# Attention and two MoE layers on one core: other places for the weight conversions, the q/k split, M's first block and the last output

## The chip, the core and the metric

The kernel runs on one core of a Trainium2 chip. The metric is the device time of one execution in microseconds (us). The median of three runs before the change is 732.38 us (731.66 to 733.02).

Five engines work in parallel, each with its own queue of instructions that it takes in order: PE (TensorE, matmuls), DVE (VectorE), ACT (ScalarE), POOL (GpSimd) and SP (SyncE), which here issues the DMAs. An instruction that waits holds up everything behind it in its queue.

## The reference

```python
# attention: B=4, H=8, S=576, D=64
cum = np.cumsum(np.maximum(s, 0.0), axis=-1)
bias = -(cum[:, :, :, None] - cum[:, :, None, :])
scores = np.where(causal, -1e9, q @ k.T / 8 + np.minimum(bias, 0.0))
attn = softmax(scores) @ v
# first MoE: 2304 tokens of 512, DF=1024
x = attn.reshape(2304, 512)
h = (x @ w1) * (x @ w2) @ w3
x = h @ w_out
# second MoE
h = x @ w_in
solu = h * softmax(h)
ln = (solu - mean(solu)) / sqrt(var(solu) + 1e-6) * g_ln
out = ln @ w_out2
```

All is float32. Accuracy is kept by splitting a float32 number into a high and a low word and adding three products (high x high, high x low, low x high).

## The kernel before

**Stages.** From 0 to some 390 us attention and the products of the first MoE with w1 and w2 run together. The program is written in 36 steps. A step takes one head h: its scores (`qk_part`, one large tile of 576 columns with `lmask` and four smaller ones of 448, 64, 320 and 192 with `wmask`), whose row maxima DVE takes out of PSUM (L186) and whose exponentials ACT takes (L190); the normalisation (`normalise`, L218 to L228); the transposes of head h-2 (`tr_part`) with evictions to PT (L93 on ACT, L95 on DVE); and, every other step, the product with v (`av_parts`). Steps 8 and 9 have no head, steps 10 and 11 no transposes. From step 10 on, blocks of the first MoE fill the step (`ab_unit`): block a = x@w1 for 128 of the 1024 columns f and half a batch, twelve matmuls of 128x288, copied to a_sb by ACT (L315), and block b = x@w2, which DVE multiplies by a_sb into g_sb (L323). PSUM tiles of one 512-column bank come from a pool (from step 11 on psF, six banks), those of two banks from another (psE).

**Weights.** The weights come as raw words. A chunk of 512 KB is loaded into one of two `stage` buffers (L384). Its conversion (`to_f32`, `split_w`) is s0 on ACT (L340), three passes on DVE (L346, L347, L351), the high word on ACT (L93, W<-stage) and the low word on DVE (L98, W<-stage,W). A buffer is free for the next load when the low word is written. The chunks come in the order w1(0), w2(0), w1(1), w2(1), ..., of the column blocks f = 0 to 7. `pump(n)` issues n conversions; `PUMP` says how many in which step: one in steps 3, 5, 6 and 16, two in each of steps 10 to 15. After that come chunks of w_in and of the last w_out (steps 22 to 33).

**q and k.** For heads from 8 on `split_qk(h+1)` splits q and k of the next head into words: ACT writes the high word (QK<-qk), SP copies it (L159), POOL subtracts (L98, 64x1152).

**Order.** The program is recorded and then put into the engines' queues by a scheduler that takes what is ready by its own estimates, the earlier written first. `tc.issue_after(i)` holds an instruction back until i has been issued. A conversion is held back behind the instructions in `behind`: before, the maximum and the exponential of the step's large score tile.

**Later stages.** From 390 us M = w3 @ w_out is formed in eight blocks (`m_unit`, 24 matmuls of 128x512), from w3's chunks, whose words are w3h and w3l. M's PSUM tiles come from a pool opened when psF is closed, that is when the last g_sb has been read out of it. DVE and ACT write M's words MH and ML, and convert the words of w_in's combinations (IB11 to IT4) and of g. Then x = M.g, the second MoE's h (`h_pair`), the norm, and the output (`out_unit`, 48 matmuls of 128x512, L836; a tile of 128 rows is evicted by ACT, L841, and sent off by SP, L842).

## Time and profile before

| what | value |
|---|---|
| median of 3 runs | 732.38 us |
| the profiled execution | 732.8 us, its span 731.1 us |
| mean granted clock of PE | 0.995 |
| DVE, ACT | 507.7 us (69%), 470.4 us (64%) |
| POOL | 95.2 us (13%) |
| PE idle in 20 to 40, 40 to 60 us | 0.55, 2.28 us |
| 60 to 80, 80 to 100, 100 to 120, 120 to 140 us | 0.29, 2.19, 0.24, 2.62 us |
| 140 to 380 us | 0 of 240 |
| 380 to 400, 400 to 420, 420 to 440 us | 2.24, 0, 0.61 us |
| 440 to 700 us | 0 of 260 |
| DMA share in 400 to 420 us | 1.03 (380 GB/s) |

The span is the stretch from the first to the last event of the profiled execution; 1.7 us of its time lie around it. The idle times are 20 us, or the window, less PE's busy time in it. PE's busy time counts overlapping matmuls once. The granted clock is the share of PE's full speed that it was given in a window; its levels are 1.2 and 2.4 GHz. "Idle before" in a row is the time in which the engine stood just before the instruction, and behind the arrow is what ended it.

### The profile page before, as it was taken

The numbers are of one execution on the slowest core, as the hardware profiler recorded it, in microseconds if no ns is written. First come the engines' busy times: TensorE is split into PE (matmuls) and PEld (weight loads), VectorE is DVE, ScalarE is ACT, GpSimd is POOL, SyncE is SP. The second block draws the span as 40 slices with busy tenths as digits, with TensorE's granted clock in tenths as the row PEclk, the third lists the DMA queues.
The fourth block names the chain that finished last, engine by engine and source line by source line (L and its number), as shares of the span: only waits on it lengthen the run. The fifth ranks groups of instructions, "written<-read, shape, count | busy, mean of one in ns | idle before, by whom it ended". The sixth has DMA issues, their size and how long they took to land.

```text
span 731.1 us, 12896 instructions
## 1 busy us (share of the span) xinstructions
PE 714.2 (98%) x4618; PEld 631.5 (86%) x4618; DVE 507.7 (69%) x1251; ACT 470.4 (64%) x977; POOL 95.2 (13%) x88
## 2 busy tenths in 40 slices
PE   9989998999999999999998999999999999999997
PEld 6669888889899999999997889988888988888886
DVE  7996989898777887822777966675747366563651
ACT  7996878798676777822544735576737465563742
POOL 3051322234121221000000000001000000000000
PEclk9999999999999999999999999999999999999999
DMA  5644555555476655514566933153324252302311
GB/s 124 190 135 132 156 164 146 164 148 127 140 205 184 207 164 175 179 62 161 185 204 201 378 114 101 59 116 87 79 66 102 45 133 68 87 19 68 66 36 43
DMA packets 79827, 95.50 MB, mean 131 GB/s; under 512 B 41418, under 2 KB 52682, under 8 KB 79764
## 3 DMA queue, kind: packets, MB, share of 16 engines
q1 hardware_dynamic: 79764, 94.69, 44.5%
q8 instruction: 36, 0.59, 0.3%
q14 instruction: 27, 0.22, 0.1%
HBM read 59.04 MB, written 20.14 MB: 108 GB/s over the span
## 4 chain that ended last, share of the span: by engine, by line
PE 81%; DVE 9%; DMA 5%; ACT 2%; issue 2%; SPq 0%; DVEq 0%; ACTq 0%
PE x L710 14%; PE o L836 14%; PE a L303 12%; PE b L303 11%; PE av L275 6%; PE hX L742 5%; PE tr L247 5%; DMA stage<-in_w_dram 4%; PE hZ L742 3%; PE sc L178 2%; PE sc L177 2%; PE hW L742 2%; PE hY L742 2%; DVE stage L351 2%; PE sc L169 1%
## 5 line engine op out<-in xcount | busy, mean ns | idle before, releaser
L190 ACT ACTIVATE P<-P,STAT 64x64 f32<-64x64 f32 (+4 forms) x160 | 88.5, 556 | 22.9 <-DVE STAT L186 22.3
L98 POOL TENSOR_TENSOR QK<-qk,QK 64x1152 fp32r<-64x1152 f32 x24 | 66.2, 2759 | 172.9 <-ACT QK L93 172.8
L710 PE MATMUL x<-gl,MH 128*128 128x256 f32 x288 | 80.4, 279 | 0.0
L710 PE MATMUL x<-gh,ML 128*128 128x256 f32 x288 | 80.2, 279 | 0.0
L710 PE MATMUL x<-gh,MH 128*128 128x256 f32 x288 | 79.9, 279 | 0.0
L303 PE MATMUL b<-xT0h,W 128*128 128x288 f32 x256 | 58.4, 301 | 3.5 <-DVE W L98 2.1
L303 PE MATMUL a<-xT0h,W 128*128 128x288 f32 x256 | 59.2, 306 | 0.0
L247 PE MATMUL tr<-ident,P 128*128 128x128 f32 x416 | 54.4, 275 | 3.5 <-DVE STAT L186 2.7
L303 PE MATMUL a<-xT1h,W 128*128 128x288 f32 x256 | 57.6, 300 | 0.0
L836 PE MATMUL o<-OH,lh 128*128 128x512 f32 x144 | 57.0, 396 | 0.2 <-DVE ll L98 0.2
L836 PE MATMUL o<-OH,ll 128*128 128x512 f32 x144 | 57.0, 396 | 0.0
L836 PE MATMUL o<-OL,lh 128*128 128x512 f32 x144 | 57.0, 396 | 0.0
L303 PE MATMUL b<-xT1h,W 128*128 128x288 f32 x256 | 56.4, 295 | 0.0
L710 PEld LDWEIGHTS x<-gl,MH 128*128 128x128 f32 x288 | 54.1, 188 | 1.5 <-DVE gl L98 0.2
L710 PEld LDWEIGHTS x<-gh,MH 128*128 128x128 f32 x288 | 53.9, 188 | 1.1
L710 PEld LDWEIGHTS x<-gh,ML 128*128 128x128 f32 x288 | 54.0, 188 | 0.9
L806 DVE COPY lt<-turned 128x2048 uint16<-128x2048 uint16 x16 | 22.0, 1373 | 45.4 <-DMA turned<-half 45.4
L247 PEld LDWEIGHTS tr<-ident,P 128*128 128x128 f32 x416 | 46.8, 141 | 5.4 <-issue 1.6
L323 DVE TENSOR_TENSOR g_sb<-b,a_sb 128x288 f32<-128x288 f32 x64 | 28.7, 450 | 31.6 <-PE b L303 21.5
L340 ACT ACTIVATE stage<-stage 128x512 f32<-128x512 f32 x56 | 37.1, 679 | 20.5 <-DMA stage<-in_w_dram 18.7
L226 ACT ACTIVATE P<-P,STAT 128x576 f32<-128x576 f32 x64 | 42.7, 717 | 10.5 <-DVE STAT L219 10.4
L315 ACT ACTIVATE a_sb<-a 128x288 f32<-128x288 f32 x64 | 25.7, 403 | 36.3 <-PE a L303 36.0
(191 smaller groups left out, 1984.1 us busy)
## 6 DMA issues: line engine op xcount, KB each, us to landing
stage<-in_w_dram SPq DMA_DIRECT2D x32, 512.0 KB
g_scr<-g_sb SPq DMA_DIRECT2D x32, 288.0 KB
stage<-in_wo_dram SPq DMA_DIRECT2D x16, 512.0 KB
qk<-in_qk_dram SPq DMA_DIRECT2D x24, 288.0 KB
QK<-QK SPq DMA_DIRECT2D x24, 288.0 KB
gl<-g_scr SPq DMA_DIRECT2D x24, 256.0 KB
wf<-wf_scr SPq DMA_DIRECT2D x22, 256.0 KB
out_dram<-o SPq DMA_DIRECT2D x18, 256.0 KB
```

Of the source, the lines that this page charges most:

```text
L98: eng.tensor_tensor(out=dst, in0=src, in1=hi_.bitcast(F32), op=ALU.subtract)
L190: ex = nc.scalar.activation(out=dst, in_=dst, func=AF.Exp, bias=st[0:rows, ti:ti + 1], scale=-1.0, accum_out=st[0:rows, 5 + ti:6 + ti],)
L226: nc.scalar.activation(out=dst, in_=src, func=AF.Copy, scale=r)
L247: last_tr[0] = nc.tensor.transpose(ps[:, 128 * n:128 * n + 128], pt[:, o:o + 128], ident)
L275: nc.tensor.matmul(st["ps"][64 * e:64 * e + 64, 448 + c0:448 + c1], vr[:, j, e], PT[(2 * p + e) % 4][:, o + c0:o + c1], **kw,)
L303: nc.tensor.matmul(ps, w_[:, c, fs], x_[:, c, sl], start=(c == 0 and w_ is WH and x_ is XH), stop=(c == KC - 1 and w_ is WL),)
L315: ab_last[0] = nc.scalar.activation(out=a_sb, in_=ps, func=AF.Copy).ins
L323: ab_last[1] = nc.vector.tensor_tensor(out=g[:, sl], in0=ps, in1=st["a"], op=ALU.mult).ins
L340: nc.scalar.activation(out=high.bitcast(F32), in_=high.bitcast(F32), func=AF.Copy, scale=2.0 ** -112)
L710: last = nc.tensor.matmul(ps[:, a], w_[:, k, m * 128:m * 128 + 128], g_[:, k % 2], start=(k == 0 and w_ is MH and g_ is GH), stop=(k == KF ...
L742: last_h[0] = nc.tensor.matmul(ps, x_[:, k], w_[:, k], start=first and k == 0 and x_ is XH and w_ is WH, stop=k == 1 and x_ is XL, skip_gr ...
L836: nc.tensor.matmul(ps, l_[:, k], w_[:, k], start=(k == 0 and l_ is LH and w_ is OH), stop=(k == KF - 1 and l_ is LL),)
```

## The change

There are four edits.

- **Conversions.** `behind[0]` is now the maximum of the last score tile of the step so far. The step's first conversion is written behind all score tiles (it was written behind the large one), the others behind the transposes, and these are held back behind the last two evictions of transposes (`last_ev`), one on each of ACT and DVE, instead of the score maximum.
- **Split.** `split_qk(h+1)` is written ahead of the scores of head h instead of at the end of the step.
- **M.** The first block of M takes its PSUM tile from psE, which stays open; psE is now kept at the right end and is closed before the second MoE, where psG, with the tiles X and Y of `h_pair`, takes its banks.
- **Output.** The last tile of 128 rows is computed, evicted and sent in two halves of 256 columns.

```diff
     def hi(dst, src, eng=None):
         if eng is None:
-            nc.scalar.activation(out=dst, in_=src, func=AF.Copy)
-        else:
-            eng.tensor_copy(out=dst, in_=src)
+            return nc.scalar.activation(out=dst, in_=src, func=AF.Copy)
+        return eng.tensor_copy(out=dst, in_=src)
...
         if ti == 0:
             behind[:] = [mx.ins, ex.ins]
+        behind[0] = mx.ins
...
         def evict(dst, src):
             cnt[0] += 1
-            hi(dst, src, PCOPY[cnt[0] % len(PCOPY)])
+            last_ev[cnt[0] % 2] = hi(dst, src, PCOPY[cnt[0] % len(PCOPY)]).ins
...
         if st == 11:
             ps_ctx.close()
             PSP[:] = [
-                ps_ctx.enter_context(tc.tile_pool(name="psE", bufs=1, space=PSUM)),
+                big_ctx.enter_context(tc.tile_pool(name="psE", bufs=1, space=PSUM, side="right")),
                 ps_ctx.enter_context(tc.tile_pool(name="psF", bufs=6, space=PSUM)),
             ]
...
             if NQ <= h + 2 < NH:
                 load_head(h + 2)
+            if h + 1 < NH:
+                split_qk(h + 1)
             qk_part(h, 0)
-        if st > 1:
-            pump(PUMP.get(st, 0))
-        if h is not None:
             qk_part(h, 1)
             qk_part(h, 2)
+        slots = PUMP.get(st, 0)
+        if slots:
+            pump(1)
         F(FS)
         if h is not None:
             normalise(h)
         if ph is not None:
             for part in range(4):
                 tr_part(ph, part)
+        if slots > 1:
+            behind[:] = last_ev
+            pump(slots - 1)
...
-            if h + 1 < NH:
-                split_qk(h + 1)
             if h + 3 < NQ:
...
     def m_unit(f):
-        ps = smalltile("m")
+        ps = smalltile("m") if f else bigtile("m")[:, 0]
...
     ps_ctx.close()
-    PSP[:] = [
-        ctx.enter_context(tc.tile_pool(name="psC", bufs=1, space=PSUM)),
-        ctx.enter_context(tc.tile_pool(name="psD", bufs=4, space=PSUM)),
-    ]
+    psp = {}
+    psp["Z"] = psp["W"] = ctx.enter_context(tc.tile_pool(name="psC", bufs=1, space=PSUM))
+    PSP[1] = ctx.enter_context(tc.tile_pool(name="psD", bufs=4, space=PSUM))
...
     def out_unit(t):
         LH, LL = lt_t.pop(t)
-        ps = smalltile("o")
-        for k in range(KF):
...
+        last = None
+        for c0, c1 in ((0, DM),) if t < NT - 1 else ((0, DM // 2), (DM // 2, DM)):
+            ps = smalltile("o")[:, 0:c1 - c0]
+            with ExitStack() as order:
+                if last is not None:
+                    order.enter_context(tc.issue_after(last.ins))
+                for k in range(KF):
+                    for l_, w_ in ((LH, OH), (LH, OL), (LL, OH)):
+                        last = nc.tensor.matmul(
+                            ps, l_[:, k], w_[:, k, c0:c1],
+                            start=(k == 0 and l_ is LH and w_ is OH), stop=(k == KF - 1 and l_ is LL),
+                        )
+            nc.scalar.activation(out=o[:, c0:c1], in_=ps, func=AF.Copy)
+            nc.sync.dma_start(out=out[t * 128:t * 128 + 128, c0:c1], in_=o[:, c0:c1])
...
+    big_ctx.close()
+    psp["X"] = psp["Y"] = ctx.enter_context(tc.tile_pool(name="psG", bufs=1, space=PSUM, side="right"))
```

What this makes of the queues is shown at three places on DVE, in the stretch from 70 to 120 us. In the names, stage_n is a buffer with a chunk, W01 and W11 are low words of w1, W03 and W13 low words of w2, sc_n a score tile, tr_n a transposed one.

The first place, DVE before, behind the second g_sb of the first MoE: stage_758 holds w2(2), stage_766 holds w1(3).

```order
L323 TENSOR_TENSOR g_sb_814<-b_843,a_sb_829 128x288
L186 ISA P_898,STAT1_117<-sc_899,lmask_109 128x576
L186 ISA STAT1_117 128x1
L346 TENSOR_SCALAR stage_758<-stage_758 128x512
L323 TENSOR_TENSOR g_sb_886<-b_873,a_sb_871 128x288
L347 SCALAR_TENSOR_TENSOR stage_758<-stage_758 128x512
L346 TENSOR_SCALAR stage_766<-stage_766 128x512
```

The same place after; stage_779 holds w2(2), stage_839 holds w1(3).

```order
L325 TENSOR_TENSOR g_sb_809<-b_843,a_sb_824 128x288
L348 TENSOR_SCALAR stage_839<-stage_839 128x512
L325 TENSOR_TENSOR g_sb_886<-b_873,a_sb_871 128x288
L349 SCALAR_TENSOR_TENSOR stage_839<-stage_839 128x512
L353 SCALAR_TENSOR_TENSOR stage_839<-stage_839 128x512
L186 ISA P_901,STAT1_117<-sc_902,lmask_109 128x576
```

The first pass over a chunk came from w2(2), behind a large maximum; it now comes from w1(3), ahead of it, and a g_sb follows.

The second place, DVE before, where the low word of w2(2) is written.

```order
L186 ISA STAT2_118 128x1
L186 ISA P_956,STAT2_118<-sc_989,wmask_108 128x192
L186 ISA STAT2_118 128x1
L351 SCALAR_TENSOR_TENSOR stage_766<-stage_766 128x512
L98 TENSOR_TENSOR W03_125<-stage_758,W02_124 128x4x128
L323 TENSOR_TENSOR g_sb_886<-b_1013,a_sb_1011 128x288
```

The same after; stage_933 holds w2(3).

```order
L186 ISA P_1128,STAT3_119<-sc_1129,lmask_109 128x576
L186 ISA STAT3_119 128x1
L219 TENSOR_SCALAR STAT2_118<-STAT2_118 128x5
L220 RECIPROCAL STAT2_118<-STAT2_118 128x5
L349 SCALAR_TENSOR_TENSOR stage_933<-stage_933 128x512
L229 TENSOR_SCALAR P_959<-P_959,STAT2_118 128x320
L229 TENSOR_SCALAR P_959<-P_959,STAT2_118 128x192
L98 TENSOR_TENSOR W03_125<-stage_779,W02_124 128x4x128
L353 SCALAR_TENSOR_TENSOR stage_933<-stage_933 128x512
L229 TENSOR_SCALAR P_959<-P_959,STAT2_118 64x64
L95 COPY PT0_112<-tr_1051 128x128
L325 TENSOR_TENSOR g_sb_1091<-b_1078,a_sb_1036 128x288
```

The low word of w2(2) stood ahead of the g_sb of b_1013. It now stands behind that g_sb (b_1008 in the new names, which stands eight rows above this piece), behind a large maximum and behind the second pass over w2(3), and ahead of the g_sb of the next block.

The third place, DVE before, at the first pass over w1(6) (stage_1147); stage_1139 holds w2(5).

```order
L186 ISA P_1390,STAT1_117<-sc_1423,wmask_108 128x192
L186 ISA STAT1_117 128x1
L218 TENSOR_SCALAR STAT0_116<-STAT0_116 128x5
L347 SCALAR_TENSOR_TENSOR stage_1139<-stage_1139 128x512
L219 RECIPROCAL STAT0_116<-STAT0_116 128x5
L346 TENSOR_SCALAR stage_1147<-stage_1147 128x512
L351 SCALAR_TENSOR_TENSOR stage_1139<-stage_1139 128x512
```

The same after, where stage_1198 holds w1(6), stage_1160 w2(5) and stage_1074 w1(5).

```order
L348 TENSOR_SCALAR stage_1160<-stage_1160 128x512
L98 TENSOR_TENSOR W11_127<-stage_1074,W10_126 128x4x128
L325 TENSOR_TENSOR g_sb_1286<-b_1343,a_sb_1301 128x288
L186 ISA P_1224,STAT0_116<-sc_1225,lmask_109 128x576
L186 ISA STAT0_116 128x1
L348 TENSOR_SCALAR stage_1198<-stage_1198 128x512
L325 TENSOR_TENSOR g_sb_1386<-b_1373,a_sb_1371 128x288
L186 ISA P_1393,STAT1_117<-sc_1401,wmask_108 128x448
```

The first pass over w1(6) stood behind the four smaller score tiles and the second pass over w2(5). It now stands ahead of these and of a g_sb, three instructions behind the low word of w1(5).

On PE the new order writes two matmuls of the b block of f = 2, then a whole a block, and then the other ten. M's first block stands directly behind the last b block, as before, but no longer shares a pool with it. The third block's ML and one low word of T3 (IT3l) change places with passes over w3 on DVE.

## Rows read from the trace of the kernel before

**Rows 1.** The page, part 1: busy us, share of the span, instructions by engine.

```profile
PE 714.2 (98%) x4618; PEld 631.5 (86%) x4618; DVE 507.7 (69%) x1251; ACT 470.4 (64%) x977; POOL 95.2 (13%) x88
```

**Rows 2.** Timeline of PE: start us, us, engine, line, op, tiles, [idle before <-releaser].

```profile
73.42 0.47 PE L177 MATMUL sc<-QK 128*128 128x448 f32 x1 [0.29 <-DVE g_sb L323]
...
83.53 0.40 PE L303 MATMUL b<-xT0h,W 128*128 128x288 f32 x1 [0.67 <-DVE g_sb L323]
...
85.22 0.29 PE L303 MATMUL a<-xT0h,W 128*128 128x288 f32 x1
...
89.03 0.39 PE L177 MATMUL sc<-QK 128*128 128x320 f32 x1
...
89.61 0.38 PE L247 MATMUL tr<-ident,P 128*128 128x128 f32 x2
...
92.67 0.52 PE L247 MATMUL tr<-ident,P 128*128 128x128 f32 x3 [1.40 <-DVE STAT L186]
...
120.53 0.40 PE L303 MATMUL b<-xT0h,W 128*128 128x288 f32 x1 [0.76 <-ACT W L93]
...
123.70 0.54 PE L303 MATMUL b<-xT0h,W 128*128 128x288 f32 x2 [2.09 <-DVE W L98]
...
391.99 0.50 PE L626 MATMUL m<-WOH,w3h 128*128 128x512 f32 x1 [2.24 <-DVE g_sb L323]
...
428.71 0.50 PE L626 MATMUL m<-WOH,w3h 128*128 128x512 f32 x1 [0.61 <-ACT w3h L93]
```

**Rows 3.** Windows of 4 us: length, busy us by engine, PEclk, DMA share, GB/s.

```profile
92.00:96.00 4.00, 3.21 (x15) 3.00 (x16) 4.00 (x14) 3.95 (x11) 2.03 (x1) 0.74 0.36 109
...
124.00:128.00 4.00, 4.00 (x21) 4.00 (x20) 4.00 (x19) 3.61 (x9) 0.00 (x0) 0.58 0.77 219
```

**Rows 4.** Timeline of DVE, 72 to 123 us: weight chunks and g_sb.

```profile
72.58 0.43 DVE L346 TENSOR_SCALAR stage<-stage 128x512 uint32<-128x512 uint32 x1 [1.90 <-DMA stage<-in_w_dram]
...
73.93 0.43 DVE L346 TENSOR_SCALAR stage<-stage 128x512 uint32<-128x512 uint32 x1
...
87.37 0.69 DVE L98 TENSOR_TENSOR W<-stage,W 128x512 fp32r<-128x512 f32 x1
...
91.42 0.43 DVE L346 TENSOR_SCALAR stage<-stage 128x512 uint32<-128x512 uint32 x1 [0.59 <-DMA stage<-in_w_dram]
...
109.64 0.69 DVE L98 TENSOR_TENSOR W<-stage,W 128x512 fp32r<-128x512 f32 x1 [0.84 <-ACT W L93]
...
111.26 0.45 DVE L323 TENSOR_TENSOR g_sb<-b,a_sb 128x288 f32<-128x288 f32 x1
...
116.59 0.43 DVE L346 TENSOR_SCALAR stage<-stage 128x512 uint32<-128x512 uint32 x1 [1.72 <-DMA stage<-in_w_dram]
...
116.94 0.68 DVE L351 SCALAR_TENSOR_TENSOR stage<-stage 128x512 uint32<-128x512 uint32 x1
...
122.97 0.68 DVE L98 TENSOR_TENSOR W<-stage,W 128x512 fp32r<-128x512 f32 x1
```

**Rows 5.** Timeline of POOL and of DVE, 119 to 123 us.

```profile
119.86 2.64 POOL L98 TENSOR_TENSOR QK<-qk,QK 64x1152 fp32r<-64x1152 f32 x1 [5.71 <-ACT QK L93]
...
120.74 2.31 DVE L351 SCALAR_TENSOR_TENSOR stage<-stage 128x512 uint32<-128x512 uint32 x1
```

**Rows 6.** Timeline of SP: the load of w1(6).

```profile
110.72 0.36 SPq L384 DMA_DIRECT2D stage<-in_w_dram  x1
```

**Rows 7.** Timeline of DVE and ACT, 410 to 429 us.

```profile
410.36 0.43 DVE L346 TENSOR_SCALAR stage<-stage 128x512 uint32<-128x512 uint32 x1 [0.47 <-DMA stage<-in_w_dram]
...
424.52 0.68 DVE L98 TENSOR_TENSOR IT3l<-wf,IT3h 128x512 fp32r<-128x512 f32 x1
...
427.98 0.68 ACT L93 ACTIVATE w3h<-stage 128x512 fp32r<-128x512 f32 x1 [0.85 <-DVE stage L351]
```

**Rows 8.** Timeline of ACT at the end; groups by form on ACT.

```profile
727.40 0.60 ACT L841 ACTIVATE o<-o 128x512 f32<-128x512 f32 x1 [5.00 <-PE o L836]
...
L93 ACT ACTIVATE PT<-tr 128x256 f32<-128x256 f32 x32 | 12.0, 374 | 0.0
```

More of the change, by code (lines that the diff above doesn't have):

```diff
@@ L63, in tile_attention_moe @@
     ps_ctx = ExitStack()
+    big_ctx = ExitStack()
     PSP = [
@@ L261, in tile_attention_moe @@
     last_tr = [None]
+    last_ev = [None, None]
     cnt = [0]
@@ L851, in h_pair @@
         h0, h1 = ln_t[t0][0], ln_t[t1][0]
-        X, Y, Z, W = (PSP[0].tile([128, HD], F32, tag=n, name=f"h{n}") for n in "XYZW")
+        X, Y, Z, W = (psp[n].tile([128, HD], F32, tag=n, name=f"h{n}") for n in "XYZW")
         h_mm(X, "A11", "B11", True)
```

7 lines of the change are left out of this document (removed).

## The prediction

> **What bounds the kernel now.** I read the page first. TensorE (PE) is busy for 714.2 of 731.1 us, so only PE's idle places can be won or lost [rows 1]. The second view is PE's timeline, row by row where a bracket stands. Up to 52 us DVE and ACT are full and have the same work ahead of each of PE's waits after the change, so I leave that stage as it is. Behind it there are seven places that the change can touch: 0.29, 0.67, 1.40, 0.76 and 2.09 us between 73 and 124 us, 2.24 us at 392 and 0.61 us at 428.71 [rows 2]. The third is the granted clock in 4 us windows. It stands at 0.74 in 92 to 96 and at 0.58 in 124 to 128, right behind the idle places of 92.67 and 123.70: for part of these windows PE ran at 1.2 instead of 2.4 GHz [rows 3]. From 0.58, half clock lasted (1 - 0.58) x 4 / 0.5 = 3.4 us and cost half of that, 1.7 us. The 2.24 us at 392 brought no fall that the page's slices show, so a wait's length does not tell it alone, and I price the clock in the bounds only.
>
> The fourth view is VectorE's (DVE's) timeline, to see what made PE wait. Two things do. The first instruction of a weight chunk (L346) waits for the chunk's DMA, and whatever stands behind it in DVE's queue waits too: at 91.42 it waited 0.59 us, and the score maxima behind it are what PE wanted at 92.67 [rows 4]. And DVE is slow while GpSimd (POOL) splits q and k: the L351 at 120.74 took 2.31 us beside the split of 119.86 to 122.50, and the chunk's last instruction, for which PE waited, came at 122.97 [rows 4, 5].
>
> I name chunks by weight and block: w2(2) is the chunk of w2 for the third block, f = 2. PE needs w1(f) and then w2(f), in the order of f.
>
> **The conversions, 57 to 124 us.** No conversion is added or removed; in steps 10 to 15 there are two in a step, and their places change.
>
> First, the order of the pair. Before, w2(2) was converted ahead of w1(3). Now the step's second conversion stands behind evictions only, step 11 has none of its own, and w1(3) goes first, though SP still issues w2(2)'s load ahead of w1(3)'s. In the trace, the first of these two loads released DVE at 72.58, the second at 73.93 [rows 4]. DVE's queue now meets the later one first, with g_sb behind it, for which PE waited at 73.42. So g_sb moves by up to 73.93 - 72.58 = 1.35 us.
>
> More comes from w2(2) itself. PE uses its low half in the block that began at 83.53. Now the low half is written behind the next step's large maximum and one more pass of w2(3), next to the place where w1(3)'s low half stood, 87.37 to 88.06 [rows 4]. PE goes on with two matmuls of the block and the next block meanwhile (the new order puts them there). A block took 85.22 - 83.53 = 1.69 us [rows 2]. At 88.06 there remain ten of twelve matmuls, 1.41 us, and before they would have been reached at 85.22 + 1.69 - 1.41 = 85.5. PE is late by 2.6 us there; the bounds are 0 (w2(2) is written where it was) and 2.6 + 2.64, one split of POOL in the way [rows 5].
>
> Second, w1(4). Its first instruction waited for the load until 91.42. It now stands ahead of a g_sb (0.45 us by its row at 111.26, some 0.4 where instructions overlap) and a low half (0.69 at 87.37, some 0.6), and the maxima stand behind all three. So PE can go on at about 92.67 + 0.4 + 0.6 = 93.7, if the load lands as before; coming 2.6 us late it would be there at 92.67 - 1.40 + 2.6 = 93.9. The old wait swallows most of the lateness, and about 1.2 us are left. Bounds: -1.4 (the wait vanishes) to +5.
>
> Third, w2(5), for which PE waited at 120.53 and 123.70. Before, w1(6)'s first instruction came behind a g_sb, four maxima and more, and still waited 1.72 us for its DMA, issued at 110.72 and landed at 116.6 [rows 4, 6]. That load can start only when w1(5)'s low half is written, since there are two buffers. Now the instruction stands three places behind that low half. If the load lands at the same time, all that ran from 111.26 to 116.59 - 1.72 = 114.87 (g_sb, four maxima, the sum's reciprocal, w2(5)'s second pass) runs behind it: 3.6 us. w2(5)'s third pass, at 116.94 before, comes 3.6 us later, and its high and low halves with it. The low half also gets one large maximum more ahead of it and one pass less, which is even. PE gets 0.58 us of score matmuls into the wait (89.03 to 89.61 are the same shapes) [rows 2]. So PE goes on 3.6 - 0.6 = 3.0 us later than at 123.70. PE waits for DVE's chain there, so the 1.2 us of before are in this, not beside it.
>
> What hides how much of this is open. For it speaks that w1(5)'s high half no longer stands behind an a_sb copy on ScalarE (ACT), so the 0.84 us that DVE waited for it at 109.64 may go and the load of w1(6) start as much earlier; against it, that w2(5)'s first instruction, which waits for a DMA, now stands ahead of that low half. I take the full +3.0. The bounds: below, every wait of 73 to 124 us goes, 0.29 + 0.67 + 1.40 + 0.76 + 2.09 = 5.2, and both half-clock stretches, 3.4, together -8.6; above, 3.0 plus one blocked split, +5.6.
>
> **Splitting q and k at the step's head.** The same number of splits (POOL's part 2.64 us each) start earlier; SP's copy goes with them. It costs nothing by itself: POOL is busy 13% of the span (its share on the page's first line) [rows 1]. What it moves is the stretch in which DVE is slow. The row at 120.74 shows a DVE pass with two SBUF inputs beside POOL's split: 2.31 us, where such a pass took 0.68 at 116.94 [rows 4, 5]. The Trainium skill, "SBUF — State Buffer", section "Who interferes with whom", says that a DVE instruction with two SBUF inputs and a GpSimd instruction that reads SBUF share a port pair, and that the first to issue keeps it for its whole length; the trace agrees with its 2.31 us. By it an earlier split frees nothing: it only blocks other passes. I count no gain for it; with a gain at 120.74 of 2.31 - 0.68 = 1.6 the sum would be 1.6 lower.
>
> **M's first block.** It no longer waits for the last g_sb, so PE starts 2.24 us earlier [rows 2]. What is late next is w3: at 428.71 PE waited for w3h, written at 427.98 to 428.66, so an early start alone would only lengthen that wait. In the new order two DVE instructions that stood ahead of that chunk's third pass are elsewhere: the ML of the third block is written before DVE's wait for a load at 410.36, and one low half of T3 goes behind. Each takes 0.68 us, some 0.6 where they overlap, in a stretch where DVE runs back to back [rows 7]. So w3h comes 1.2 us earlier, and PE with it: -1.2. Bounds: 0 and -(2.24 + 0.61) = -2.85. Behind 429 us PE has no idle place up to 715, so the gain holds to the end.
>
> **The last output.** Two halves of 256 columns. The PE time stays (48 matmuls half as long). The last eviction took 0.60 us for 512 columns; for 256 columns from PSUM the evictions to PT have 0.374 [rows 8]: -0.2. The last transfer has half the bytes; from the eviction's end at 728.0 to the end of the span pass 3.1 us, and no row splits them into fixed and by size. I take 0.15 (bounds 0 and 1.5). Together -0.35.
>
> **The sum.** +3.0 - 1.2 - 0.35 = +1.45 us on the profiled 732.8 us, thus 734.25; on the runs' median of 732.38, 0.4 below, 733.8. I forecast about that.
>
> **The rivals.**
> - The load chain runs ahead (faster). w1(6)'s load starts and lands before DVE gets to it, and w2(5) is on time: the 0.76 and 2.09 of 120 to 124 go, and one half-clock stretch, 1.7; of the earlier places 0.29 and 0.67 go and 1.2 stays. That is -5.5 + 1.2 = -4.3, with the other terms -5.85: 726.5. It decides if the load has landed when DVE comes to the instruction: behind the low half DVE has only a g_sb and a large maximum to do, some 1.2 us, and otherwise waits for PE. Against it stand the 5.9 us from issue to landing at 110.72.
> - M gains nothing, because w3 comes with its loads alone: +3.0 - 0.35, 735.0. For it: DMA is what DVE waits for at 410 us.
> - The splits get in the way again. They now start when w1(3)'s low half or the pass behind it is due. One blocked pass, 2.64 - 0.68 = 2.0 us, on top of the sum: 735.8. The rule of the Trainium skill's page "SBUF — State Buffer" ("Who interferes with whom") would have it so wherever both run at once.
> - The early stage comes out even: lateness at 88 is swallowed by the wait of 92.67, and w2(5) comes as late as before. -1.2 - 0.35: 730.8.
>
> **How the numbers follow.** The forecast 0.28; chain ahead 0.22; M without gain 0.20; a split in the way 0.14; even 0.16. A measurement of this kernel can tell about 0.2%, 1.46 us, from no change, so 730.9 to 733.8 counts as the same. The forecast lies on that edge: 0.15 of it slower, 0.12 the same. M without gain and the split are nearly all slower, 0.32; the chain ahead is faster, and of the even case 0.12. That gives faster 0.35, same 0.18, slower 0.47. The forecast's own range is 732 to 736. As cases of both signs hold most of the chance, the range for 8 in 10 goes from 726.0 to 738.0.
>
> **What would show it.** In the new trace: PE's wait for w2(2)'s low half near 88 us (about 2.5 us, in the middle of a block); the wait of 92.67 short; DVE idle for several us on the first instruction of w1(6), with g_sb and maxima behind it, and PE's wait for w2(5) ending near 127. M's first matmul directly behind the last b, a wait of 1 to 2 us for w3h in its place, and the end of the last transfer 3.4 us behind the last matmul. The prediction is wrong if PE's idle time of 57 to 130 us shrinks, if w1(6) finds its data there, or if the half-clock stretches go.

## The result and the profile after

The changed kernel takes 739.21 us (median of six runs, 737.2 to 740.8), the kernel before 732.7 beside it (731.28 to 734.47). The ratio is 1.0088 [1.0065, 1.0111]: slower by 6.5 us. The prediction had the side (slower) and not the size: it said +1.45 us, 733.8, in a range of 726 to 738. The profiled execution took 740.22 us, its span 738.5. Single executions of 872 us and more occur below (one of e2, one of e15, one of the kernel before): they stand in the medians and not in the ratios, and of e2, whose profiled execution is such a one (4012 us), only the order of the queues is read.

The page's first line of the changed kernel (columns as in [rows 1]):

```profile
PE 717.2 (97%) x4642; PEld 634.0 (86%) x4642; DVE 511.6 (69%) x1251; ACT 469.9 (64%) x978; POOL 95.8 (13%) x88
```

PE has 24 more matmuls, from the last output's halves, and is busy 3.0 us longer; the other 4.4 of the 7.4 us by which the span grew are idle time of PE. DVE has as many instructions as before and is busy 3.9 us longer. The places where PE was idle, which answer to [rows 2] (PE's timeline: start, length, line, operation, tiles, count, idle before and what ended it):

```profile
49.42 1.10 PE L169 MATMUL sc<-QKN 128*128 128x320 f32 x4 [2.57 <-DVE STAT L186]
77.42 0.47 PE L177 MATMUL sc<-QK 128*128 128x512 f32 x1 [2.74 <-issue]
90.14 0.40 PE L305 MATMUL b<-xT0h,W 128*128 128x288 f32 x1 [0.44 <-ACT W L94]
93.90 0.54 PE L305 MATMUL b<-xT0h,W 128*128 128x288 f32 x2 [0.96 <-DVE W L98]
100.66 0.43 PE L177 MATMUL sc<-QK 128*128 128x320 f32 x1 [0.33 <-DVE STAT L186]
123.77 0.47 PE L177 MATMUL sc<-QK 128*128 128x512 f32 x1 [1.16 <-issue]
125.22 0.40 PE L305 MATMUL a<-xT0h,W 128*128 128x288 f32 x1 [0.61 <-ACT a_sb L317]
128.06 0.47 PE L177 MATMUL sc<-QK 128*128 128x448 f32 x1 [0.73 <-DVE g_sb L325]
146.69 0.42 PE L177 MATMUL sc<-QK 128*128 128x320 f32 x1 [0.96 <-DVE g_sb L325]
157.82 0.40 PE L305 MATMUL a<-xT0h,W 128*128 128x288 f32 x1 [0.72 <-DVE g_sb L325]
432.79 0.50 PE L631 MATMUL m<-WOH,w3h 128*128 128x512 f32 x1 [1.77 <-ACT w3h L94]
433.84 0.79 PE L631 MATMUL m<-WOH,w3h 128*128 128x512 f32 x1 [0.32 <-ACT w3h L94]
455.10 0.50 PE L714 MATMUL x<-gh,MH 128*128 128x256 f32 x2 [0.49 <-ACT gh L94]
```

New or grown are the places at 49 and 77 us and those of 146 and 157 us. The 2.24 us ahead of M are gone; 2.09 us of waits for w3h stand inside M instead. The granted clock, which answers to [rows 3] (windows of 4 us, columns as there):

```profile
76.00:80.00 4.00, 2.58 (x13) 2.50 (x14) 3.44 (x10) 1.37 (x2) 0.00 (x0) 0.84 0.02 8
80.00:84.00 4.00, 4.00 (x22) 3.87 (x22) 4.00 (x16) 3.92 (x9) 2.71 (x1) 0.73 0.38 80
124.00:128.00 4.00, 2.72 (x18) 2.29 (x17) 4.00 (x7) 3.96 (x10) 3.33 (x1) 1.00 0.37 80
432.00:436.00 4.00, 2.90 (x10) 2.27 (x11) 4.00 (x8) 1.41 (x3) 0.00 (x0) 0.72 0.64 173
436.00:440.00 4.00, 4.00 (x28) 3.88 (x28) 1.39 (x3) 0.67 (x1) 0.00 (x0) 0.86 0.02 6
```

There are two stretches at half clock, as before, each costing about 1.7 us (for the last: (0.28 + 0.14) x 4). They only stand elsewhere: behind the wait of 77.42 and inside M.

**How late PE is, place by place.** I count the matmuls of a kind (a, b, x) in two timelines and compare when the same one starts. A positive lag is later than in the trace of before. The first column of lags is two kernels measured below whose order is exactly that of before (e10; e6 up to M): theirs is what one execution differs from another. (e4 and e12, whose order up to M is that of before too, lie between -0.4 and 1.0 up to there.) Where a kernel takes its blocks in another order, a lag contains that order as well: the change's goes from 5.3 at 115 us to 8.1 at 117 and back to 6.4 at 120.

| at us | same order | whole change | steps 3, 5, 6 (e7) | steps from 10 (e8) | second chunk (e16) | bank shift (e5) |
|---|---|---|---|---|---|---|
| 59 | 0.7, 0.8 | 2.8 | 3.4 | 0.9 | 0.1 | 1.1 |
| 77 | 0.7, 0.8 | 6.8 | 3.1 | 2.2 | 1.0 | 2.0 |
| 115 | -0.5, -0.3 | 5.3 | 3.4 | 3.0 | -0.5 | 6.7 |
| 139 | -0.8, -0.7 | 3.7 | 1.5 | 1.6 | -1.0 | 6.4 |
| 188 | 1.0, -0.8 | 5.8 | 3.4 | 4.6 | 4.7 | 6.3 |
| 390 | 1.0, -0.8 | 5.9 | 3.4 | 4.8 | 4.7 | 6.6 |
| 483 | 1.7 | 7.8 | 2.5 | 4.6 | 3.6 | 6.0 |

Against the same-order kernels the whole change loses 2.1 us by 59 us and some 4 more by 77 us; about 1.6 come back by 139 us; 0.3 to 2.1 are lost by 188 us (e10 loses 1.8 there itself), 1.9 in M; and 0.4 come back at the end (+7.4 at the span's end).

### The profile page after: what moved, and what is told of

It reads as the page before. It is cut to its first block, busy times and chain, and to the rows that moved or that the text cites. A ratio compares the mean times of both kernels' runs of the same rounds, so it can differ in the third digit from the quotient of the medians.

```text
span 738.5 us, 12949 instructions
## 1 busy us (share of the span) xinstructions
PE 717.2 (97%) x4642; PEld 634.0 (86%) x4642; DVE 511.6 (69%) x1251; ACT 469.9 (64%) x978; POOL 95.8 (13%) x88
## 4 chain that ended last, share of the span: by engine, by line
PE 73%; DVE 13%; DMA 8%; ACT 3%; issue 2%; DVEq 0%; ACTq 0%; SPq 0%
PE o L846 13%; PE x L714 13%; PE a L305 10%; PE b L305 10%; DMA stage<-in_w_dram 7%; PE hX L746 5%; PE av L277 4%; PE tr L248 4%; PE hZ L746 3%; DVE P L186 3%; DVE stage L349 2%; DVE stage L353 2%; PE sc L178 2%; PE hW L746 2%; PE hY L746 2%
## 5 line engine op out<-in xcount | busy, mean ns | idle before, releaser
L190 ACT ACTIVATE P<-P,STAT 128x576 f32<-128x576 f32 (+4 forms) x160 | 88.3, 554 | 23.9 <-DVE STAT L186 23.3
L846 PE MATMUL o<-OH,lh 128*128 128x512 f32 (+1 forms) x152 | 58.4, 384 | 0.2 <-DVE ll L98 0.2
L846 PE MATMUL o<-OH,ll 128*128 128x512 f32 (+1 forms) x152 | 58.3, 384 | 0.0
L846 PE MATMUL o<-OL,lh 128*128 128x512 f32 (+1 forms) x152 | 58.3, 383 | 0.0
L349 DVE SCALAR_TENSOR_TENSOR stage<-stage 128x512 uint32<-128x512 uint32 x56 | 49.9, 900 | 2.1 <-ACT stage L342 1.4
L177 PE MATMUL sc<-QK 128*128 128x448 f32 (+3 forms) x144 | 43.8, 317 | 5.9 <-issue 3.9
```

The lines of the kernel that those rows point to most:

```text
L177: nc.tensor.matmul(view, t[:, 0, q0:q0 + rows], t[:, 3, c0:c0 + w], start=True, stop=False)
L190: ex = nc.scalar.activation(out=dst, in_=dst, func=AF.Exp, bias=st[0:rows, ti:ti + 1], scale=-1.0, accum_out=st[0:rows, 5 + ti:6 + ti],)
L349: nc.vector.scalar_tensor_tensor(out=low, in0=high, scalar=3, in1=low, op0=ALU.logical_shift_left, op1=ALU.bitwise_or,)
L846: last = nc.tensor.matmul(ps, l_[:, k], w_[:, k, c0:c1], start=(k == 0 and l_ is LH and w_ is OH), stop=(k == KF - 1 and l_ is LL),)
```

## The experiments

All are edits of the kernel before, unless said otherwise. Times are medians beside the kernel before on the same chip. DVE is its busy time by the page's first line.

| kernel | us, before | ratio | DVE us |
|---|---|---|---|
| e1 conversions alone | 738.56, 732.99 | 1.0070 [1.0047, 1.0093] | 513.6 |
| e2 split alone | 732.79, 732.99 | 0.9998 [0.9979, 1.0017] | |
| e3 M alone | 739.74, 732.99 | 1.0096 [1.0062, 1.0130] | 508.5 |
| e4 output alone | 733.56, 732.99 | 1.0006 [0.9988, 1.0023] | 507.1 |
| e5 bank shift alone | 740.11, 732.7 | 1.0108 [1.0081, 1.0135] | 511.1 |
| e6 M without the shift | 732.51, 732.7 | 0.9989 [0.9975, 1.0004] | 507.6 |
| e7 conversions, steps 3, 5, 6 | 734.55, 732.7 | 1.0025 [1.0011, 1.0039] | 507.3 |
| e8 conversions, steps from 10 | 735.87, 732.7 | 1.0037 [1.0018, 1.0056] | 513.9 |
| e9 whole change without the shift | 738.72, 732.57 | 1.0092 [1.0073, 1.0110] | 513.6 |
| e10 both large pools mirrored | 732.95, 732.57 | 1.0012 [0.9997, 1.0026] | 506.8 |
| e11 e8 with the pair's old order | 737.64, 732.57 | 1.0071 [1.0052, 1.0091] | 513.2 |
| e12 split, M without shift, output | 732.87, 732.57 | 1.0010 [0.9992, 1.0027] | 507.0 |
| e13 before, third stage buffer | 735.77, 732.66 | 1.0044 [1.0026, 1.0061] | 509.5 |
| e14 e8, third stage buffer | 735.37, 732.66 | 1.0036 [1.0022, 1.0050] | 512.3 |
| e15 whole change, third stage buffer | 738.85, 732.66 | 1.0081 [1.0060, 1.0102] | 515.1 |
| e16 second chunk alone | 738.50, 732.66 | 1.0092 [1.0064, 1.0121] | 510.4 |
| e17 conversions, steps 10 to 13 | 734.10, 732.84 | 1.0020 [0.9991, 1.0048] | 509.6 |
| e18 conversions, steps 14 to 16 | 732.85, 732.84 | 0.9998 [0.9985, 1.0012] | 506.9 |

### The four parts alone

```diff
e1: -  pump(PUMP.get(st, 0))            # behind the large score tile
    +  pump(1)                          # behind the last maximum
    +  behind[:] = last_ev; pump(slots - 1)
e2: split_qk(h + 1) from the step's end to its head
e3: +  big_ctx, psE with side="right"; m_unit(0) in bigtile("m"); psG behind M
e4: +  for c0, c1 in ((0, DM // 2), (DM // 2, DM))   # the last out_unit
```

> Only the conversions' new places, on the kernel before. Theory A (the conversions are the main cost: the chunk loaded second is converted first, DVE waits for its load with g_sb behind it, and PE stands for it near 75 us; and conversions in the first 54 us delay score maxima): +3 to +5 us, with a DVE wait of 3 us or more for a load near 75 us and a PE wait of 2 us or more behind it. Rival B (the earlier splits are the main cost): within 1.5 us of before.

> Only the q/k split at the step's head. Theory A: 0 to +2 us, from passes that POOL's splits block. Rival B: +4 to +6 us, with PE waits behind blocked DVE instructions in 40 to 160 us.

> Only M's first block in the kept bank. Theory A: M's matmuls start 2.2 us earlier, PE then waits 1.5 to 2 us for w3h near 427 us and runs at half clock for some 3 us behind it: -0.5 to +1 us in all. Rival B, as the prediction had it: -1.2 us, and no half clock.

> Only the last output in two halves. Theory A and rival B alike: -0.2 to -0.7 us; from the last matmul's end to the end of the span 3.2 us instead of 3.8.

The split and the output do nothing that can be measured. The split alone doesn't even change an order: in e2 every engine takes the same instructions one after the other as before. The conversions alone cost nearly the whole loss (+5.6, above theory A's +3 to +5), and so does M alone (+6.75, outside both theories), though together the parts cost little more than each. The trace of e3 puts M's loss where M is not: its lag is 4.6 us at 96 us and 7.4 at 136.

### What M's edit does at step 11

The edit opens psE, the pool of the large score tile from step 11 on, on the other side of PSUM. e5 has this alone, and e6 has M's edit without it:

```diff
e5: -   ps_ctx...tile_pool(name="psE", bufs=1, space=PSUM)
    +   ps_ctx...tile_pool(name="psE", bufs=1, space=PSUM, side="right")
e6: -   big_ctx...tile_pool(name="psE", ..., side="right")   # as in the change
    +   big_ctx...tile_pool(name="psE", ...)                 # psC, psD on the right, psG on the left
```

> The kernel before with one keyword more: psE, the pool of the large score tile from step 11 on, is opened on the right side of PSUM, so that it takes banks 6 and 7 (the old psB's) and psF takes 0 to 5 (the old psA's and two of psB's), where before psE lay over psA and psF over psB. No edit of M. Theory 'banks': the loss of the M edit alone (+6.7 us, of which the profile shows 4.6 by 96 us and 7 by 136 us, hundreds of us ahead of M) comes from the pool change of step 11: the large score tile has to wait for the last users of the small tiles' banks, so scores and maxima stand later in every queue. Then this kernel loses +5 to +7.5 us, 738 to 740, PE waits beyond 2 us near 88 and 127 us as in the M edit alone, and is even from 140 us on. Rival 'M': the loss comes of M's block or its later pools, then it is at 732.7 +/- 1.5.

> The M edit with psE left where it was (banks 0 and 1), and the pools that follow M opened on the right side in its place; the order up to M is that of the kernel before. Theory 'banks': no early loss; M's first block starts directly behind the last b (2.24 us earlier), then 1.5 to 2.1 us of waits for w3h stand in M, and half a clock behind them costs 1 to 1.7 us: together -1 to +1.5 us, 732 to 734. The prediction's own term for M was -1.2: 731.5. Rival 'M': still +6 us, 739.

One keyword costs 7.4 us, and M without it is at -0.2 us (-0.8 by the ratio). Before, psE lay over banks of the old large tiles; shifted, it lies over banks that held small tiles (scores, a and b), and the order puts the large score tile of step 11 behind one more a and b block of twelve matmuls each. In the trace of before it started at 68.51 us:

```profile
68.51 0.39 PE L177 MATMUL sc<-QK 128*128 128x512 f32 x1
```

In e5 it starts at 74.07, when the g_sb that reads the last b is written (PE's timeline, then DVE's and POOL's):

```profile
74.07 0.47 PE L177 MATMUL sc<-QK 128*128 128x512 f32 x1 [0.67 <-issue]
88.58 0.37 PE L303 MATMUL b<-xT0h,W 128*128 128x288 f32 x1 [3.76 <-DVE P L228]
...
73.51 0.46 DVE L323 TENSOR_TENSOR g_sb<-b,a_sb 128x288 f32<-128x288 f32 x1 [2.41 <-PE b L303]
...
79.67 2.90 DVE L347 SCALAR_TENSOR_TENSOR stage<-stage 128x512 uint32<-128x512 uint32 x1
83.16 3.72 DVE L351 SCALAR_TENSOR_TENSOR stage<-stage 128x512 uint32<-128x512 uint32 x2
...
79.02 2.99 POOL L98 TENSOR_TENSOR QK<-qk,QK 64x1152 fp32r<-64x1152 f32 x1 [14.23 <-ACT QK L93]
83.31 3.03 POOL L98 TENSOR_TENSOR QK<-qk,QK 64x1152 fp32r<-64x1152 f32 x1 [1.29 <-ACT QK L93]
```

The large maximum of the step starts at 74.95 instead of 69.92, that of the next step at 82.48 instead of 74.28; the smaller ones come at about their old time (76.31, before 75.56). The conversions now stand among and behind these and meet POOL's splits (2.90 us for a pass that took 0.68 at 116.94 [rows 4]; before, a low half met them too, for 3.14 us), and the normalisation for which PE waits 3.76 us stands behind those. e10 asks whether the side or the overlap does it: psA goes to the right too, so that psE lies over the old large tiles again.

```diff
-   tile_pool(name="psA", bufs=2, space=PSUM)
+   tile_pool(name="psA", bufs=2, space=PSUM, side="right")   # and psE on the right, as in e5
```

> The kernel before with psA and psE both opened on the right: the large score tile of step 11 lies again over banks of the old large tiles, though on the right side; no other edit. Theory 'overlap': what cost 7.4 us in the bank shift alone was whose old banks psE takes over, not the side: 732.7 +/- 1.2, PE's large score tile of step 11 at its old place near 68.5 us. Rival 'side': banks 6 and 7 themselves are slow: 736 or more.

No loss: it is the overlap. e9 takes the shift out of the whole change.

```diff
-   big_ctx...tile_pool(name="psE", ..., side="right")   # in the change; psC, psD, psG as in e6
+   big_ctx...tile_pool(name="psE", ...)
```

> The whole change with one thing taken back: psE is opened on the left (banks 0 and 1, as before), M's later pools on the right. The parts measured alone: conversions +1.85 (steps 3, 5, 6) and +3.2 (steps from 10 on), together +5.6; split 0; M without the bank shift -0.2 (-0.8 by the ratio); output 0; bank shift +7.4. Theory 'conversions carry it': the bank shift's loss and the conversions' stand on the same waits of 77 to 136 us, so that of the shift's 7.4 only 1 to 2 us are left once the conversions are moved: 737 to 738.5. Rival 'shift carries it': the parts add up, then taking 7.4 from 739.2 gives 731.8.

The first theory held, just above its range: without the shift the whole change is at 738.72, with it at 739.21, and the intervals overlap. In e9 PE waits 0.28 us at 75.69 where the change waits 2.74 us at 77.42, and its lag at 77 us is 2.3 us instead of 6.8; but at 188 us the two are at 5.0 and 5.8.

### Which conversions cost

```diff
e7: steps 3, 5, 6 as in the change;      if st >= 10: pump(PUMP.get(st, 0))   # old place
e8: steps from 10 on as in the change;   if 1 < st < 10: pump(PUMP.get(st, 0)) # old place
```

> Of the conversion edit only the steps ahead of step 10 (one chunk each in steps 3, 5 and 6: its first pass stands behind the step's last maximum); from step 10 on as before. The whole edit alone was +5.6 us, its profile 2.6 us late at 49 us. Theory 'three stages': +1.5 to +3 us from the first 54 us, carried to the end: 734.2 to 735.7, PE waiting some 2.6 us for a score maximum near 49 us. Rival 'swallowed': the lateness of the start is taken back by waits of the next stage: 732.7 +/- 0.8. The prediction counted nothing in the first 52 us.

> Of the conversion edit only the steps from 10 on; steps 3, 5 and 6 as before. Theory 'three stages': +3 to +4.5 us, 735.7 to 737.2, of which about 1 to 2 by 136 us, 2 to 3.5 between 140 and 190 us (waits for g_sb behind a chunk's first pass, which waits for its DMA), and up to 2 around M (waits for w3h). If the first 54 us carried the whole: 732.7 +/- 0.8. The prediction's own working had +3.0 between 57 and 124 us and nothing later: 735.7.

+1.85 and +3.2: both stages cost, the second as much as the prediction had for it (+3.0). e7's wait is that of the change at 49.42:

```profile
49.03 1.29 PE L168 MATMUL sc<-QKN 128*128 128x320 f32 x4 [2.58 <-DVE STAT L185]
```

In e7's trace a half-clock stretch lies behind that wait (0.73 in 48 to 52 us, 0.85 in 52 to 56, some 1.7 us), in the change's none. DVE of the changed kernel, in the order of e7, shows what stands ahead of the maxima that PE waited for, the first of which began at 48.54:

```profile
43.12 0.71 DVE L186 CUSTOM_DVE_ANT_0 P<-sc,lmask 128x576 f32<-128x576 f32 x1
43.76 2.54 DVE L349 SCALAR_TENSOR_TENSOR stage<-stage 128x512 uint32<-128x512 uint32 x1
46.22 0.68 DVE L98 TENSOR_TENSOR W<-stage,W 128x512 fp32r<-128x512 f32 x1
47.35 0.68 DVE L353 SCALAR_TENSOR_TENSOR stage<-stage 128x512 uint32<-128x512 uint32 x1
48.54 0.58 DVE L186 CUSTOM_DVE_ANT_0 P<-sc,wmask 128x448 f32<-128x448 f32 x1
```

Behind the large maximum of 43.12 the chunk's second pass, low half and third pass come before the small maxima. Before, the third pass alone stood between the two:

```profile
40.91 0.71 DVE L186 CUSTOM_DVE_ANT_0 P<-sc,lmask 128x576 f32<-128x576 f32 x1
42.16 2.36 DVE L351 SCALAR_TENSOR_TENSOR stage<-stage 128x512 uint32<-128x512 uint32 x1
...
46.56 0.61 DVE L186 CUSTOM_DVE_ANT_0 P<-sc,wmask 128x448 f32<-128x448 f32 x1
```

Yet from the large maximum to the first small one it is 5.42 us after and 5.65 before: this stretch got no longer, and the large maximum itself is late (2.2 us, of which this execution has 0.9 at 20 us already). The time is lost further ahead, where DVE stands idle after and had a pass of the chunk to do before (DVE after, then before):

```profile
25.59 0.76 DVE L186 CUSTOM_DVE_ANT_0 P<-sc,lmask 128x576 f32<-128x576 f32 x1 [0.85 <-PE sc L169]
33.78 0.35 DVE L95 COPY PT<-tr 64x192 f32<-64x192 f32 x1 [1.68 <-PE tr L248]
...
31.32 0.69 DVE L347 SCALAR_TENSOR_TENSOR stage<-stage 128x512 uint32<-128x512 uint32 x1 [0.77 <-ACT stage L340]
```

Between 20 and 48 us DVE is busy 24.82 us in the change and 24.84 in e7, but 26.78 before and 26.50 in e10. The passes that filled its waits for PE now stand where it has none.

The pair's order, the first step of the prediction's working, is put back in e11:

```diff
e11: in e8:  behind[:] = last_ev   ->   if ph is not None: behind[:] = last_ev   # steps 10, 11 keep w2(2) first
```

> The conversions of the steps from 10 on as in the change (735.9 alone), but w2(2) stays ahead of w1(3): in steps 10 and 11, which have no evictions of their own, the second chunk keeps the wait for the step's last maximum. Theory of the prediction (the swapped pair): DVE meets the earlier load first, g_sb moves back by 1.35 us at 74 us and w2(2) is on time at 88; what it saves there is partly given back, -1 to -2.5 us: 733.4 to 734.9. Rival: the chunks are late because their first passes stand behind the step's last maximum, and the pair's order does not matter: 735.9 +/- 0.8.

The theory fell. DVE's wait for w1(3) goes, and the lag at 77 us falls from 2.2 to 0.9, but the kernel is no faster: its median is 1.8 us above e8's, with intervals that just touch. Its PE waits longer behind that:

```profile
86.67 0.37 PE L304 MATMUL b<-xT0h,W 128*128 128x288 f32 x1 [2.88 <-DVE g_sb L324]
100.67 0.40 PE L304 MATMUL b<-xT0h,W 128*128 128x288 f32 x1 [1.63 <-ACT W L93]
124.35 0.81 PE L247 MATMUL tr<-ident,P 128*128 128x128 f32 x3 [3.41 <-DVE g_sb L324]
```

### Is it the loads?

DVE of the changed kernel waits for chunk loads, above all at these two places, as the prediction had it (DVE's timeline):

```profile
76.52 0.43 DVE L348 TENSOR_SCALAR stage<-stage 128x512 uint32<-128x512 uint32 x1 [4.23 <-DMA stage<-in_w_dram]
118.51 0.80 DVE L348 TENSOR_SCALAR stage<-stage 128x512 uint32<-128x512 uint32 x1 [2.68 <-DMA stage<-in_w_dram]
119.23 0.45 DVE L325 TENSOR_TENSOR g_sb<-b,a_sb 128x288 f32<-128x288 f32 x1
```

A load starts when one of two buffers is free. e13, e14 and e15 add a third to the kernel before, to e8 and to the change; e16 splits the pair.

```diff
e13 to e15: -  stg = [at, 2]
            +  stg = [at, 3]
e16: in steps from 10 on the first chunk stays where it was, the second goes behind the last evictions
     +  if st > 1: pump(PUMP.get(st, 0) if st < 10 else min(1, PUMP.get(st, 0)))   # old place
```

> The kernel before with three staging buffers for weight chunks up to the end of the attention stage (two before), so that a chunk's load is issued one chunk earlier. No edit of the change. Theory 'load chain': what the conversions wait for is the load of their own chunk, which starts only when a buffer is free; then DVE's waits for staged chunks between 57 and 124 us go, and PE's waits of 88 to 124 us with them: -1.5 to -5 us, 728 to 731. Rival 'queue order': the loads are not what ends last, the chunks' places in DVE's queue are: 732.7 +/- 1.5.

> The conversions of the steps from 10 on as in the change (735.9 with two staging buffers, where DVE waits 3.7 us for a chunk's load at 74.8 us and 0.4 to 1.6 us at five more chunks up to 128 us), with three buffers. Theory 'load chain': the +3.2 us are those waits, and go: within 1 us of the kernel before with three buffers. Rival 'queue order': the +3.2 stay on top of that kernel's time, since maxima and g_sb stand behind the conversions whether the data is there or not.

> The whole change with three staging buffers. Theory 'load chain': of the change's +6.5 us the part from 57 us on goes (3.2 and more); left are +1.9 of steps 3, 5 and 6 and what the bank shift costs by itself: 734 to 736.5. Rival 'queue order': 738.5 to 740.

> Of the conversions of the steps from 10 on only the second of each step is moved, behind the step's last evictions; the first stays at its old place, between the large maximum and the small scores. Theory 'first passes': the +3.2 us of both together come from the first chunk's place behind the step's last maximum, so this kernel is at 732.7 +/- 1. Rival 'second': the second chunk, which comes later in the step than its consumer can bear, carries them: 735 to 736.5.

The load chain does not decide the time. The third buffer makes the kernel before slower by 3.1 us, which neither theory had, and leaves e8 and the change where they were. (e14 is within 1 us of e13, as the load-chain theory said, but only because e13 is as slow.) Up to 135 us the loads do count: between 57 and 135 us PE is idle 3.78 us in e14 and 6.81 in e8, and 5.78 in e15 against 7.10 in the change; behind, from 135 to 200 us, e14 gives back 0.7 and e15 1.0 of that. e14's profiled execution (733.65) was near its kernel's fastest, so its trace shows more of a gain than its median. In e13 DVE waits less for loads between 57 and 124 us (1.54 + 1.03 us, before 1.90 + 0.96 + 0.59 + 1.72), so the buffer does what it should. But conversions that come earlier stand ahead of the g_sb for which PE waits (PE, then DVE and POOL of e13, then DVE of before):

```profile
86.55 0.40 PE L303 MATMUL b<-xT0h,W 128*128 128x288 f32 x1 [2.14 <-DVE g_sb L323]
...
82.06 3.13 DVE L98 TENSOR_TENSOR W<-stage,W 128x512 fp32r<-128x512 f32 x1
86.05 0.45 DVE L323 TENSOR_TENSOR g_sb<-b,a_sb 128x288 f32<-128x288 f32 x1
...
77.70 6.94 POOL L98 TENSOR_TENSOR QK<-qk,QK 64x1152 fp32r<-64x1152 f32 x2 [13.04 <-ACT QK L93]
...
79.97 3.14 DVE L98 TENSOR_TENSOR W<-stage,W 128x512 fp32r<-128x512 f32 x1
83.03 0.45 DVE L323 TENSOR_TENSOR g_sb<-b,a_sb 128x288 f32<-128x288 f32 x1
```

The low half beside the split is as long before (3.14 us) as in e13 (3.13). What is new in e13 is one more low half and two more first passes between the large maximum and that g_sb: 10.00 us from the one (76.05) to the other, before 8.75 (from 74.28). PE waits 2.14 us there, before 0.67 [rows 2]. e13's lag is 1.8 us at 115 us, that of the same-order kernels -0.5 and -0.3.

e16 costs +5.8, more than both chunks together (+3.2), so the cost doesn't lie on one of them. By its lag it is even with before until 139 us and loses all behind that (PE, DVE, and a window):

```profile
143.80 0.44 PE L176 MATMUL sc<-QK 128*128 128x448 f32 x1 [2.62 <-issue]
...
141.87 0.43 DVE L346 TENSOR_SCALAR stage<-stage 128x512 uint32<-128x512 uint32 x1 [1.36 <-DMA stage<-in_w_dram]
...
144.00:148.00 4.00, 4.00 (x19) 3.97 (x19) 4.00 (x7) 2.52 (x7) 2.63 (x1) 0.58 0.35 74
```

### The steps from 10 on in two pieces

```diff
e17: if 1 < st < 10 or st > 13: pump(...)   # old place; steps 10 to 13 as in the change
e18: if 1 < st < 14 or st > 16: pump(...)   # old place; steps 14 to 16 as in the change
```

> The conversions of steps 10 to 13 alone moved as in the change (in the kernel before, 57 to about 108 us); steps 14 to 16 and all others as before. The prediction's own working: w2(2) late by 2.6 us at 88, 1.2 us of it left behind the wait of 92.67, and that swallowed by PE's wait for w2(5) at 123.70, which does not move here: 0 to +1.2 us, 732.7 to 733.9. Theory 'steps 10 to 13 carry it' (the lateness of 2 us at 77 us goes on to the end): +2 to +3.5 us, 734.7 to 736.2, with e18 near 733.

> The conversions of steps 14 to 16 alone moved as in the change (in the kernel before, from about 108 us); all others as before. The prediction's own working: w1(6)'s first pass ahead of g_sb and four maxima, PE 3.0 us later at 123.70 and nothing behind it: 735.7. Theory 'behind 124 us': PE's wait near 124 us stays about as long, and the loss of 2 us and more comes between 139 and 160 us, where the kernel before has no wait of PE and the whole change has two, of 0.96 and 0.72 us, and where the second-chunk edit alone waited 2.6 us at 143.8 with a granted clock of 0.58 behind it: 734.5 to 736, lag below 1 us at 139 us and 2 or more at 187.

e17 is at +1.3, just above the 0 to 1.2 that the prediction's working gives for these steps, though its interval takes in zero. e18 is even, against +3.0 and against both theories. PE waits there for w2(5) as long as before (2.11 us; 2.09 in [rows 2]):

```profile
124.61 0.54 PE L304 MATMUL b<-xT0h,W 128*128 128x288 f32 x2 [2.11 <-DVE W L97]
```

This bears on the +3.0 less than I wanted: with steps 10 to 13 unmoved, w1(6)'s first pass is taken at 117.50 us, where it was, and not ahead of the maxima as in the whole change. So e18 shows that steps 14 to 16 cost nothing alone, and the two medians make up 1.3 of the 3.2 us. As e17's interval reaches from -0.7 to +3.5 us, it is not shown that the two cost less apart than together.

### What is harmless, together

e12 is the whole change with conversions as before and psE on the left.

```diff
in e9:  -  pump(1) behind the last maximum, pump(slots - 1) behind last_ev
        +  if st > 1: pump(PUMP.get(st, 0))   # old place
```

> What the runs have found harmless, together: split at the step's head, M's first block in the kept bank with psE on the left, the output in two halves; conversions as before. Sum of the measured parts: 0 (split), -0.2 to -0.8 (M), +0.4 to -0.3 (output): 731.6 to 732.9. If the split's move costs once M is earlier (POOL's splits of the last heads lie in 350 to 390 us): up to 734. The prediction's terms would make it -1.55: 731.2.

No difference, and no kernel of these beats the kernel before by more than its measurement can tell; e6 is nearest (-0.8 us by the ratio).

## Why the prediction was wrong in size

- **"Up to 52 us ... I leave that stage as it is": failed, +1.85 us (e7).** I took DVE and ACT as full and their work as the same. The work was, its order was not, and DVE was not full: it had waits for PE in which the chunk's passes stood. With these moved it is idle 1.7 to 2.0 us more between 20 and 48 us, the maxima come late, and PE waits 2.57 us at 49.42.
- **The pair's order: the place was right, its role wrong.** DVE did wait at the later load, 4.23 us where I had up to 1.35 for g_sb. I had taken the loads' times from before; but a load starts when a low half is written, and two low halves that stood one behind the other (from 67.97) now lie apart (68.03 and 70.87). The second load is issued 2.3 us later (SP before, then after):

```profile
68.69 0.94 SPq L384 DMA_DIRECT2D stage<-in_w_dram  x2
...
68.74 3.19 SPq L386 DMA_DIRECT2D stage<-in_w_dram  x2
```

  PE's wait of 2.74 us at 77.42 takes this wait and the bank shift together: the large score tile now needs the g_sb behind the load, and in e9, without the shift, DVE waits 2.45 us for the load too, but that tile stands ahead of it (70.79) and PE waits 0.28 us. Still, e11 shows the old order is no cheaper in the end. A wait at 77 us is no loss if the next stages end in DVE's chain anyway.
- **w2(2)'s low half: right in kind, too large.** PE waits for it in the middle of a block, 0.96 us at 93.90 (and 0.44 for a high half at 90.14), forecast 2.6.
- **w1(6) and w2(5), +3.0: near e8's +3.2 by luck.** e8's lag is 3.0 us at 115 us already (same order: -0.5 and -0.3), and near 124 us its PE waits 0.54 + 1.42 us, less than before; e18, which moves these steps alone, costs nothing. In the change DVE waited 2.68 us for w1(6)'s load with g_sb and four maxima behind it, and PE's waits ended at 128.06 (forecast near 127). But PE was 5 us late by then and waited 1.16 + 0.61 + 0.73 = 2.5 us, not more than the 0.76 + 2.09 of [rows 2]. Between 59 and 139 us the change lost 0.9 us by the lags (3.7 - 2.8), or 2.4 against the same-order kernels, whose lag fell by 1.5.
- **Nothing behind 124 us, implied by the sum: not refuted by the change, but without the ground that I gave it.** The profile of before shows PE never idle from 140 to 380 us, and I took that for slack. It is tight: an execution of the same order (e10) waited 0.63 and 0.76 us there, the change 0.96 and 0.72 us, e16 2.62 us with a half-clock stretch behind. e16's lag goes from -1.0 to 4.7 there. The change's, against the same-order kernels, is 5.7 at 115 us and 4.8 to 6.6 at 188.
- **M, -1.2: its place right, its gain not shown, and the edit as it was is more than M.** M starts directly behind the last b, and the wait for w3h takes its place, as forecast. e6 gives -1.4 in its profile (lag from -0.8 to -2.2) and -0.8 by its ratio, whose interval (-1.8 to +0.3) holds both the forecast and nothing; e12, with the same M, gains 0.5 in its profile. In the whole change the wait for w3h is 2.09 us with half a clock behind it, and 1.9 us are lost there. The edit of M does not do that by itself, since e1, which hasn't got it, also loses 1.9 (7.2 to 9.1), with 0.80 us of wait behind this one:

```profile
436.14 0.50 PE L630 MATMUL m<-WOH,w3h 128*128 128x512 f32 x1 [2.02 <-ACT w3h L93]
```

  Why w3h is late where all conversions are moved is open. What I missed is the pool: I read psE's new side as a detail of M, and it is the bank shift of step 11, +7.4 alone.
- **Split 0, output -0.35: not contradicted.** Neither can be told from zero alone. The split is zero for another reason than mine: I had POOL's splits start earlier, and e2's queues are unchanged; in the change the splits of 76.14 come at 81.29 and 87.18. For the output e4's ratio gives +0.4 (-0.9 to +1.7). In the trace the last eviction takes 0.38 us, and from its start to the span's end pass 3.26 us (before 3.70), 0.2 of it in the eviction:

```profile
735.24 0.38 ACT L850 ACTIVATE o<-o 128x256 f32<-128x256 f32 x1 [2.40 <-PE o L846]
```

So the steps that failed are two prices left at zero, the first 52 us (+1.85 by e7) and the banks of step 11 (with the late load, some 4 us at 77 us in the change); the term of 57 to 124 us, which did not arise at 124; and the gains of M and the output, which do not show (e12, with both, is at +0.3).

The parts measured alone sum to 1.85 + 3.2 + 0 - 0.2 + 7.4 + 0.6 = 12.85, and the whole is 6.5. It is the bank shift that doesn't add. The conversions do (1.85 + 3.2, and e1 measures 5.6 for both), and with the harmless parts they make e9, at +6.15. The shift adds 0.5 to that, less than the intervals can tell: its 4.5 us at 77 us (6.8, e9 2.3) are 0.8 at 188 us.

What stays open: where in the steps from 10 on the conversions cost their 3.2 us, and why e16 costs more than e8. A common sign is that DVE, with the same 1251 instructions, is busy longer: 509.5 to 515.1 us in all kernels that move conversions from step 10 on or start them earlier, but for e18, the one of these without loss (506.9), and 506.8 to 507.7 in those that are even. It does not give the size: e14 has 512.3 us and +2.7, e3 508.5 us and +6.75. DVE's passes over 128x512 with two tensor inputs that took over 1 us, 8 to 11 in each of these traces, all overlap a split on POOL. What they took above 0.68 us sums to 15.2 us before, 22.1 in e8, but 15.2 in the change and 14.9 in e13: these passes can make up e8's longer DVE time and not that of the other two. Passes that a split lengthens are the prediction's third rival, priced there at one pass of 2.0 us. By the Trainium skill, "SBUF — State Buffer", section "Who interferes with whom", a DVE instruction with two SBUF inputs contends with a GpSimd instruction that reads SBUF; the low halves of 3.13 us in e13 and 3.14 us before, which subtract one SBUF tile from another, agree. No run moved POOL's splits out of the conversions' stretch, so this cause is argued and not shown; and e7, at 507.3 us, shows that a loss can come without it.

## What to carry to other kernels

When a tile pool is opened again, look whose banks it covers: one side keyword cost 7.4 us some 300 us ahead of the code that it was written for. A stage in which the bound engine is never idle is not a stage with slack, and a stage whose order moves has to be priced even if its work does not change. Where several engines take turns at being late, edits don't add: measure each alone and all together, and price a conversion by what stands behind it in its queue and by the wait that it used to fill, not only by when its load lands.

## What the runs showed of the hardware that was not expected

- A third staging buffer cut DVE's waits for loads in 57 to 124 us from 5.17 to 2.57 us and made the kernel 3.1 us slower; the pass that POOL's split lengthens took as long as before (3.13 and 3.14 us).
- The length of PE's wait alone did not tell whether the clock fell: behind 2.57 us at 49.42 the granted clock of the change stayed at 1.00 in 48 to 56 us, behind 2.58 us at the same place (49.03) e7's was 0.73 in 48 to 52, and behind 2.62 us at 143.80 e16's was 0.58 in 144 to 148.
- Executions with the same order differ by nearly 2 us of lag (1.0 and -0.8 at 188 us), and by more where a load is late: e18, in the order of before up to 109 us, lags 2.7 us at 59 us, behind a load for which DVE waited 2.38 us at 22.81. A smaller difference in a single trace tells nothing.
